# Scatters without the small fill ahead of them, and a new order at the start of the second expert

## The chip, the cores and the metric

The kernel runs on one core of a Trainium2 chip. The metric is the device time of one execution in microseconds (us); a change is read against the median of three runs.

## The reference, cut to what matters

```
# attention: a linear recurrence with decay w, per batch and head (B=4, H=8, S=768, D=48)
for t in range(S):
    y[t]  = r[t] @ (state + (u*k[t]) outer v[t])
    state = w[t][:, None] * state + k[t] outer v[t]
# its output is x: 3072 tokens of 384 values; a router sends each token to one of 8 experts
logits = x @ w_gate;  e = argmax(logits);  g = softmax(logits)[e]
out[token] = g * (relu(x[token] @ w1[e]) @ w2[e])        # w1: 384x1024, w2: 1024x384
```

## The kernel before

**Attention.** 32 iterations (`for i in range(2, NI)`, after a hand-written start), each half a sequence of one pair of heads. The order of each engine's instructions is written by hand; the engines run their own streams in order and meet at semaphores. One iteration on GpSimd (POOL) is `rk` (L444), `diag` (L519, makes SC), `k_mul` (L497, makes Kd), one or two one-element fills that hold back a load (`pace`), in some iterations a scatter, and last `f_out` (L488), which copies 12 columns of the decay product F into `flags`, read much later to tell whether the chunked form was numerically sound. In every second iteration a one-element copy `hint` (L885) follows the scan `states` (L567, makes TT) of VectorE. VectorE runs `decay_l` (L474), `decay_f` (L482), `r_mul` (L500), `sc_out` (L532, which waits for `diag`) and `states`. `decay_l` overwrites a buffer that `k_mul` read, so it waits for GpSimd too.

**Routing.** While batch b+1 is in attention, batch b is routed: its rows are scattered by expert into the DRAM tensor `xs`, 128 rows at a time, by `route_s`: a one-element fill of `spacer` (L277), and an indirect DMA issued by GpSimd (L278). `SCAT` puts 13 of these scatters at the ends of iterations 15 to 20, 23 to 27 and 31 (two of them around the start of iteration 27), 5 behind the last iteration and 6 in the tail, when the last batch is routed. The rows are then read back for the first expert.

**Experts.** Expert 0 has two parts: its first rows are worked off in the attention's tail, the rest (256 rows) afterwards. Experts 1 to 7 (in order of their size) have 464 rows and fewer. The products are made of high and low halves (`H`, `L`) of weights and activations, three matmuls for each. `mm1(e, f)`, f = 0 to 7, makes the hidden block f in one of four PSUM banks (nine matmuls); ScalarE evicts its high half (hH, L1282), VectorE its low half (hL, L1283), and the bank is free when both are done. Then `mm2` (three blocks d, eight f each), whose f-th three matmuls need hH and hL of that f.

For the next expert, in the same time, `xload_` loads its rows (4 DMAs on the SP queue, L1230), `tags` the gate weight and row number of each (4 DMAs of 8-byte pieces, L1217), four DMAs load its weights into four staging buffers (L1057). `xturn` transposes the rows on VectorE (L1240) and `xsplit` makes their halves in three steps, one ScalarE and one VectorE instruction each (L1247, L1248). `W[e+1][2](g)` splits a quarter g of the weights in the same way (L1076, L1078). Where in expert e's blocks `xturn` and the three `xsplit` stand is in `XF`; 8 and up are the blocks of `mm2`. Quarters 0 and 1 of the next expert's w1 are split around the start of `mm2`, quarters 2 and 3 (w2) during the second and third block of `mm2`; only for expert 1 do they stand in its own `mm1`, at f = 1 and f = 4 (`late`).

The issue order on SP around the second expert: weights 0 of expert 1, its rows, weights 1, a zero fill of `xs`, weights 2 and 3, the tags of expert 1; then, with expert 1 started, the rows of expert 2, its tags, its four weights. Loads from `xs` wait for the zero fill.

## Time and profile before

| | |
|---|---|
| median of three runs | 405.98 us (405.19 to 406.72) |
| profiled execution | 406.11 us, of which 404.3 us are the span of its instructions |
| TensorE clock granted | 0.996 of full speed in the mean |
| busy: TensorE, VectorE, GpSimd, ScalarE | 380.5, 293.1, 238.5, 213.5 us |
| attention with its tail; experts | to about 188 us; from there to the end |

Busy time of TensorE contains matmuls that only keep it going (`warm`, `spin`, `pulse`), and the ends of its instructions are modelled, so a stall is read better from the starts of instructions. In a timeline the columns are start (us), duration (us), engine, line, operation, output and inputs, count, and in brackets the idle time of the engine before it and what ended that. PEld is the weight load of TensorE.

### The profile page before, as it was taken

What the parts mean: (1) busy time and instruction counts of PE and PEld (TensorE: products, weight loads), DVE (VectorE), ACT (ScalarE), POOL (GpSimd) and SP (SyncE); (2) the same over time, 40 slices, a digit from 0 to 9 for tenths busy, and PEclk for the clock granted to TensorE, in tenths of its full rate; (3) what the DMA queues carried; (4) which work ended last, traced back from release to release, by engine and by line L of the source; (5) the groups of instructions that cost most, each with busy time, mean ns of one, the idle gap of its engine ahead of it and who ended that gap; (6) DMA issues with size and microseconds to landing.
All of it is one profiled execution on the core that took longest, in us unless ns stands there. A gap on an engine that the chain in (4) does not pass through costs nothing.

```text
span 404.3 us, 13751 instructions
## 1 busy us (share of the span) xinstructions
PE 380.5 (94%) x5546; PEld 338.2 (84%) x5547; DVE 293.1 (72%) x498; ACT 213.5 (53%) x439; POOL 238.5 (59%) x469
## 2 busy tenths in 40 slices
PE   8879999999989989999999999999999999999992
PEld 4567777787767768789988799999999999999992
DVE  7688998888888876567776968787596695864510
ACT  6667668656755764454264564465455554471300
POOL 8655777669976994762120008848748488388211
PEclk9999999999999999999999999999999999999998
DMA  9999998668775954236999769757847576521001
GB/s 141 170 166 157 166 188 179 131 126 174 173 150 123 267 157 147 104 111 192 230 237 212 241 124 357 170 167 209 227 152 183 178 244 175 179 98 37 35 19 40
DMA packets 149039, 66.10 MB, mean 163 GB/s; under 512 B 127774, under 2 KB 140283, under 8 KB 148966
## 3 DMA queue, kind: packets, MB, share of 16 engines
q1 hardware_dynamic: 143030, 55.36, 59.5%
q0 software_dynamic: 4336, 9.47, 6.7%
q8 instruction: 45, 0.74, 0.8%
q10 hardware_dynamic: 1600, 0.30, 0.5%
q14 instruction: 28, 0.23, 0.2%
HBM read 49.72 MB, written 15.87 MB: 162 GB/s over the span
## 4 chain that ended last, share of the span: by engine, by line
PE 64%; DVE 10%; SPq 6%; DMA 6%; POOL 5%; issue 4%; ACT 4%; POOLq 0%; DVEq 0%; ACTq 0%
PE ps L1278 5%; PE pt L1278 5%; PE pk L1265 5%; PE pk L1266 5%; PE pw L1278 5%; PE pp L1278 5%; PE pk L1264 5%; SPq L417 4%; PE both L528 3%; DMA xg<-xs 3%; PE py L596 3%; PE py L1266 3%; PE py L1265 3%; PE py L1264 3%; DVE TT L567 2%
## 5 line engine op out<-in xcount | busy, mean ns | idle before, releaser
L1334 POOL DMA_INDIRECT out_dram<-yo,yi x68 | 85.9, 1264 | 69.4 <-DVE yo L1330 54.7
L1078 DVE TENSOR_TENSOR w2L<-wstage,w2H 128x1536 fp32r<-128x1536 f32 x16 | 33.0, 2060 | 9.1 <-ACT w2H L1076 9.1
L519 POOL TENSOR_TENSOR SC<-eye,qT 128x384 f32<-128x384 f32 x32 | 26.5, 828 | 15.9 <-ACT qT L512 15.6
L278 POOL DMA_INDIRECT xs<-xr,slu x24 | 29.0, 1207 | 8.7 <-DVE slu L272 4.3
L444 POOL TENSOR_TENSOR rk<-rT,kT 112x384 f32<-112x384 f32 x32 | 31.9, 996 | 1.9 <-ACT rT L465 1.9
L1078 DVE TENSOR_TENSOR w1L<-wstage,w1H 128x1536 fp32r<-128x1536 f32 x16 | 28.0, 1756 | 6.8 <-ACT w1H L1076 6.5
L474 DVE TENSOR_TENSOR_SCAN L<-pw,stepb 112x390 f32<-112x390 f32 x30 | 28.7, 956 | 4.6 <-PE pw L453 2.1
L1076 ACT ACTIVATE w2H<-wstage 128x1536 fp32r<-128x1536 f32 x16 | 31.5, 1977 | 0.0
L497 POOL TENSOR_TENSOR Kd<-kT,L 112x384 f32<-112x384 f32 x32 | 29.8, 932 | 1.5 <-ACT kT L469 1.5
L482 DVE TENSOR_TENSOR_SCAN F<-pw,bfw 112x390 f32<-112x390 f32 x30 | 29.0, 968 | 0.9
L516 ACT ACTIVATE Kt<-both 128x288 f32<-128x288 f32 x32 | 13.1, 410 | 31.2 <-PE both L528 30.1
L528 PE MATMUL both<-RF,Kd 48*64 48x112 f32 x768 | 27.9, 262 | 1.6 <-issue 1.6
L1265 PE MATMUL pk<-hL,w2H 128*128 128x464 f32 (+4 forms) x80 | 28.6, 357 | 0.6 <-DVE hL L1283 0.6
L1266 PE MATMUL pk<-hH,w2L 128*128 128x464 f32 (+4 forms) x80 | 28.5, 356 | 0.0
L1264 PE MATMUL pk<-hH,w2H 128*128 128x464 f32 (+4 forms) x80 | 28.4, 355 | 0.0
L532 DVE COPY_PREDICATED SC<-mask,both 128x384 f32<-128x384 uint32 x32 | 19.0, 593 | 11.4 <-POOL SC L519 5.4
L1084 POOL DMA_INDIRECT out_dram<-orow,tag x8 | 9.3, 1160 | 26.8 <-DVE orow L1355 26.3
L567 DVE TENSOR_TENSOR_SCAN TT<-PT,AT 112x576 f32<-112x576 f32 x16 | 22.8, 1425 | 1.2 <-ACT PT L562 1.2
L546 PEld LDWEIGHTS py<-V,Kt 64*48 64x48 f32 x704 | 17.1, 121 | 7.6 <-ACT qT L512 4.8
L1076 ACT ACTIVATE w1H<-wstage 128x1536 fp32r<-128x1536 f32 x16 | 23.5, 1478 | 0.0
L528 PEld LDWEIGHTS both<-RF,Kd 48*64 48x64 f32 x768 | 21.4, 134 | 2.0 <-issue 2.0
L546 PE MATMUL py<-V,Kt 64*48 64x48 f32 x704 | 22.2, 212 | 0.7 <-ACT Kt L516 0.4
(307 smaller groups left out, 1180.5 us busy)
## 6 DMA issues: line engine op xcount, KB each, us to landing
wstage<-in_moe_w_dram SPq DMA_DIRECT2D x28, 768.0 KB
xs<-zrow SPq DMA_DIRECT2D x7, 723.8 KB
in_w<-in_w_dram SPq DMA_DIRECT2D x30, 144.0 KB
in_k<-in_k_dram SPq DMA_DIRECT2D x30, 144.0 KB
in_r<-in_r_dram SPq DMA_DIRECT2D x30, 144.0 KB
V<-in_v_dram SPq DMA_DIRECT2D x15, 168.0 KB
V<-in_v_dram SPq DMA_DIRECT2D x16, 144.0 KB
xg<-xs SPq DMA_DIRECT2D x12, 156.0 KB
```

The source lines that it names most:

```text
L444: nc.gpsimd.tensor_tensor(t[:GP], T["rT", i][:GP], T["kT", i][:GP], op=OP.mult)
L497: nc.gpsimd.tensor_tensor(KDM[i % 3][:GP], chunks(T["kT", i][:GP], C), T["L", i][:, :, 1:], op=OP.mult)
L528: nc.tensor.matmul(psS[half(side, c % 2), side, c // 2, :], KDM[i % 3][kr, c, :], RF[i % 6][kr, c, :], start=True, stop=True)
L546: nc.tensor.matmul(p[64 * side:64 * side + D, par, q, :], T["Kt", i][ts, side, q, :], vat(un, side, par, h * NB + q), start=fresh, stop=fresh)
L567: nc.vector.tensor_tensor_scan(t[:GP].rearrange("p e c -> p (e c)"), PT[un % 2][:GP].rearrange("p e c -> p (e c)"), AT[un % 3][:GP].rearra ...
L1076: nc.scalar.activation(hh, sv, AF.Copy)
L1078: nc.vector.tensor_tensor(ll, sv, hh.bitcast(F32), op=OP.subtract)
L1264: nc.tensor.matmul(p, lh, rh, start=first, stop=False)
L1265: nc.tensor.matmul(p, lh, rl, start=False, stop=False)
L1266: nc.tensor.matmul(p, ll, rh, start=False, stop=last)
L1278: nc.tensor.matmul(p, ws["1" + x][:, c, sl], X[y, e][:, c, :n], start=(j == 0), stop=(j == len(terms) - 1))
L1334: d = nc.gpsimd.indirect_dma_start(out=out.rearrange("n (g x) -> (n g) x", g=XP), out_offset=bass.IndirectOffsetOnAxis(ap=X["i", e][:, q:q ...
```

## The change

Four edits. `route_s` loses the fill of `spacer` (24 times). `f_out` is done by ScalarE in place of GpSimd in those iterations in which a scatter stands. At expert 1, the tags are issued behind the rows of expert 2 in place of ahead of them, and `xturn` and `xsplit` for expert 2 stand at f = 5, 6, 7 and 8 in place of 2, 3, 4 and 5. Quarter 0 of the weights of expert 1 is split after f = 6 of expert 0's `mm1` in place of after f = 7, `xturn` and the first `xsplit`.

```
-XF = ((7,7,8,8),(2,3,4,5))
+XF = ((7,7,8,8),(5,6,7,8),(2,3,4,5))
...
     def route_s(st, q, scat):
-        nc.gpsimd.memset(spacer, 0.0)
         d = nc.gpsimd.indirect_dma_start(
...
-            def f_out(i):
+            def f_out(i, scattered=False):
                 af = flags[:GP, i * NCH * NFS:(i + 1) * NCH * NFS].rearrange("p (c x) -> p c x", x=NFS)
-                nc.gpsimd.tensor_copy(af, T["Fx", i][:, :, 0:C + 1:C // (NFS - 1)])
+                src = T["Fx", i][:, :, 0:C + 1:C // (NFS - 1)]
+                if scattered:
+                    nc.scalar.activation(af, src, AF.Copy)
+                else:
+                    nc.gpsimd.tensor_copy(af, src)
...
                 scatter(i, 1)
                 if nx:
-                    f_out(i + 2)
+                    f_out(i + 2, 2 * i in SC or 2 * i + 1 in SC)
...
             def turn(e, t):
-                for j, at in enumerate(XF[e > 0]):
+                for j, at in enumerate(XF[min(e, 2)]):
...
                     if e:
                         xload_(e + 1, X["src", e + 1])
-                        tags(e + 1, X["src", e + 1] * NR)
+                        for k in range(1 if e == 1 else e + 1, e + 2):
+                            tags(k, X["src", k] * NR)
...
                         W[1][1](2)
                         W[1][1](3)
-                        tags(1, X["src", 1] * NR)
...
                     for at, g, which in late.get(e, ()):
                         if at == f:
                             W[e][2](g, which)
+                    if (e, f) == (0, 6):
+                        W[1][2](0)
                     if nx:
                         turn(e, f)
                 if nx:
-                    W[e + 1][2](0)
+                    if e:
+                        W[e + 1][2](0)
```

## Rows read from the trace of the kernel before

**Rows 1.** Busy time of each engine in the two stretches with scatters between iterations.

```profile
87.70:113.30 25.60, 24.25 (x685) 19.38 (x678) 21.46 (x31) 17.78 (x49) 24.79 (x52) 1.00 0.78 172
127.30:150.40 23.10, 20.47 (x575) 16.34 (x568) 18.57 (x31) 15.25 (x41) 22.23 (x52) 1.00 0.76 204
```

**Rows 2.** Waits of VectorE from 87.7 to 114: total us, times, longest.

```profile
DVE SC L532 <- POOL SC L519: 2.0, 6, 0.5
```

**Rows 3.** Timeline of GpSimd around scatters.

```profile
87.59 0.20 POOL L488 COPY flags<-F 112x12 f32<-112x12 f32 x1
87.72 0.18 POOL L885 COPY hint<-TT 1x1 f32<-1x1 f32 x1
...
90.54 0.09 POOL L277 MEMSET spacer<- 1x1 f32 x1
90.79 1.02 POOL L278 DMA_INDIRECT xs<-xr,slu  x1 [0.16 <-issue]
91.82 0.20 POOL L488 COPY flags<-F 112x12 f32<-112x12 f32 x1
91.98 0.99 POOL L444 TENSOR_TENSOR rk<-rT,kT 112x384 f32<-112x384 f32 x1
...
134.77 1.99 POOL L278 DMA_INDIRECT xs<-xr,slu  x1 [0.16 <-issue]
```

**Rows 4.** Waits of TensorE's weight loads from 204 to 240.

```profile
PEld pk L1265 <- DVE hL L1283: 1.4, 2, 0.8
PEld pw L1278 <- DVE hL L1283: 1.1, 1, 1.1
PEld ps L1278 <- DVE w1L L1078: 0.6, 1, 0.6
...
PEld pk L1266 <- DVE w2L L1078: 0.3, 1, 0.3
```

**Rows 5.** Timeline of TensorE: early rows, end of expert 0, expert 1, start of expert 2.

```profile
186.56 0.52 PE L1122 MATMUL pp<-ident,xr 128*128 128x128 f32 x3 [0.32 <-DMA xr<-xs]
...
200.78 0.33 PE L1266 MATMUL pk<-w2H,hL 128*128 128x384 f32 x1
...
205.15 0.37 PE L1278 MATMUL ps<-xH,w1H 128*128 128x464 f32 x1
...
228.30 0.37 PE L1264 MATMUL py<-hH,w2H 128*128 128x464 f32 x1
...
238.37 0.36 PE L1278 MATMUL ps<-xH,w1H 128*128 128x436 f32 x1
```

**Rows 6.** Timeline of VectorE in two scatter iterations.

```profile
90.60 0.97 DVE L474 TENSOR_TENSOR_SCAN L<-pw,stepb 112x390 f32<-112x390 f32 x1 [0.30 <-POOL spacer L277]
...
134.59 1.35 DVE L567 TENSOR_TENSOR_SCAN TT<-PT,AT 112x576 f32<-112x576 f32 x1
```

**Rows 7.** Groups of ScalarE by line: busy us, mean ns, idle before.

```profile
L512 ACT ACTIVATE qT<-both 128x6 f32<-128x6 f32 x32 | 5.5, 172 | 1.1 <-PE both L528 1.1
```

**Rows 8.** Timeline of VectorE and ScalarE, experts 0 and 1.

```profile
196.67 0.42 DVE L1283 SCALAR_TENSOR_TENSOR hL<-pp,hH 128x256 fp32r<-128x256 f32 x1
...
199.79 2.14 DVE L1240 STREAM_TRANSPOSE xT<-xg 128x1440 f32<-128x1440 f32 x1 [1.99 <-DMA xg<-xs]
...
202.47 1.47 ACT L1076 ACTIVATE w1H<-wstage 128x1536 fp32r<-128x1536 f32 x1
...
203.97 1.76 DVE L1078 TENSOR_TENSOR w1L<-wstage,w1H 128x1536 fp32r<-128x1536 f32 x1 [0.72 <-ACT w1H L1076]
...
217.43 1.98 DVE L1240 STREAM_TRANSPOSE xT<-xg 128x1344 f32<-128x1344 f32 x1 [1.98 <-DMA xg<-xs]
219.33 0.60 DVE L1283 SCALAR_TENSOR_TENSOR hL<-pw,hH 128x464 fp32r<-128x464 f32 x1
...
222.66 2.27 DVE L1078 TENSOR_TENSOR w2L<-wstage,w2H 128x1536 fp32r<-128x1536 f32 x1 [1.43 <-ACT w2H L1076]
```

**Rows 9.** Timeline of the SP queue as expert 1 starts.

```profile
205.60 3.35 SPq L1217 DMA_DIRECT2D tag<-xs  x4
```

## The prediction

> **What bounds the kernel now.** I read the page's busy shares, then the chain that ended last, then each stretch that the diff touches. TensorE has by far the largest share of the chain, so most of the kernel is matmuls that no edit here shortens; what can be won are the places where TensorE stands still or where the attention loop is paced by another engine. There are two such places.

> The first is the loop while scatters run in it. The busy table of the two scatter stretches [rows 1] shows GpSimd filled: 24.79 of 25.60 us and 22.23 of 23.10, and what is missing are the short gaps ahead of each scatter. VectorE has 4.1 and 4.5 us left. TensorE looks as full as GpSimd, but part of its work there is pulses that only keep it going. Who waits decides: VectorE waits for GpSimd's SC in all six iterations of the first stretch, 2.0 us together [rows 2], and before `decay_l` 0.30 us for the buffer that `k_mul` reads [rows 6] (the fill is named there because it ended next; the reader of that buffer is Kd). So an instruction taken from GpSimd in these iterations brings SC and Kd forward, and VectorE with them, up to that wait.

> The second is expert 1. Its first matmul starts at 205.15 and that of expert 2 at 238.37 [rows 5]: 33.2 us for 144 matmuls (72 of `mm1`, 72 of `mm2`). The last 48 of them run from 228.30 to 238.37, 0.21 us each; at that pace 144 take 30.2. So 3.0 us are stalls, and the weight loads' waits name them [rows 4]: the low weights of quarter 0 and low halves hL, all VectorE's work. Why VectorE is late stands in its timeline [rows 8]: `xturn` of expert 2 stands in its stream at f = 2 and waits 1.98 us for rows that aren't there before 217.4, then takes 1.98 us, with hL of f = 3 behind it until 219.33; the four PSUM banks then hold up f = 7. And at the start, quarter 0 of w1 is split behind `xturn` of expert 1, which waited 1.99 us for its rows, so w1L comes at 203.97 + 1.76 = 205.7, later than TensorE's 205.15.

> **The change part by part.** *Flags on ScalarE.* Eleven copies leave GpSimd (iterations 15 to 20 and 23 to 27; in iteration 31 there is none to copy). What one is worth is the distance from its start to the next start: 91.98 - 91.82 = 0.16 where `rk` follows, 87.72 - 87.59 = 0.13 where `hint` follows [rows 3]. Five of the first kind and six of the second: 0.80 + 0.78 = 1.6 us. On ScalarE each costs about 0.17 us, as the copy of 6 columns does [rows 7]; 11 times 0.17 = 1.9 us. They stand at the end of an iteration, and F was made half an iteration before, so they wait for nothing; behind them are the eviction of the next transposes and then the wait for the next `sc`. ScalarE has 25.60 - 17.78 = 7.8 us free in the first stretch, so I take nothing; if that cover is gone the 1.9 us come back.

> *The fill.* It lasts 0.09 us, but instructions of GpSimd overlap at their ends. Bounds: nothing (the gap ahead of the scatter just grows) and 0.09. Of the 13 in the loop the six scatters that meet VectorE's scan of the states gain nothing: at 134.77 a scatter took 1.99 us in place of 1.02 [rows 3], and it was the scan from 134.59, 1.35 long [rows 6], that held it: 135.94 plus some 0.8 is its end. Starting earlier there only waits longer. Six others (the 13th, in iteration 31, stands where GpSimd idles) at 0.05, between the ends: 0.3. With the flags 1.9; the waits of VectorE to be won are a third of a us in an iteration [rows 2, 6] and GpSimd gives back 0.13 to 0.25, so nearly all of it can pass, but not all of it must: I take 1.7, bounds 0 and 2.2 (1.6 + 6 x 0.09).

> [...]

> *The tail.* The six last scatters run one behind another and the rows of the first expert are read back after them; TensorE then waits 0.32 us for these rows [rows 5]. Six fills are 0 to 0.5 us; I take 0.2 of the 0.32. The other five stand ahead of a pause of GpSimd: nothing.

> *Quarter 0 of expert 1 sooner.* The split of 1.47 us on ScalarE and 1.76 on VectorE [rows 8] now stands ahead of the evictions of f = 7 of expert 0. When VectorE takes f = 6's low half at 196.67 its high half is done; so w1H ends by 198.1, w1L by 199.9, hL of f = 7 by 200.3 (0.42). The matmul that needs it starts at 200.78 [rows 5], so it is 0.4 us in time or more. `xturn` of expert 1 starts at 200.3 at the latest in place of 199.79 and ends at 202.5; three steps of about 0.6 each and one eviction of `mm2` follow, to 205.0. The low halves of the rows are used last in f = 0, six matmuls after 205.15, at 206.4. So w1L no longer stalls and xL neither. The cover is that first `mm2` of 8 us; without it the split would cost its 1.76.

> *`xturn` and `xsplit` of expert 2 later.* Without stalls f = 4 ends at 205.15 + 45 x 0.21 = 214.6 and `mm2` starts at 220.3; its last low half is needed 22 matmuls on, at 224.9. ScalarE evicts f = 4 (0.6) and splits quarter 3, as long as VectorE's half, 2.27 [rows 8]: 217.5. VectorE: w2L to 219.8, hL of f = 5 (0.6), `xturn` (1.98) to 222.4, hL of f = 6 to 223.0, xL to 223.6, hL of f = 7 to 224.2. ScalarE's xH and hH of f = 7 lie beside that. That is 0.7 us in time. What is late next is the expert after: its first product now is at some 235, its third xsplit done by some 227.

> *The tags.* Four DMAs, 3.35 us of SP's time [rows 9], move behind the four of expert 2's rows, which so start some 3.4 us sooner than behind them; these were waited for until 217.4, and now nobody asks before 220. Behind the tags are expert 2's tags and its four weights: the same DMAs are ahead of those as before, so they move by nothing, and the last weight's buffer, freed by the split of quarter 3, comes free 5 us sooner (219.8 against 222.66 + 2.27). Expert 1's tags are first used after the first block of `mm2`, about 225, and are issued by about 213.

> For the two edits at expert 1 the stalls of 3.0 us are the upper bound; I take 2.8, as a few evictions may still be met. The lower bound is 1.5, if the start is won only half and one low half is late by its 0.6.

> **Sum.** 406.1 (the profiled execution's own time, 0.1 above the median) - 1.7 - 0.2 - 2.8 = 401.4 us. After expert 1 TensorE runs without a wait into the last expert, so what is won there stays.

> **Rivals.** *A: as summed*, 400.4 to 402.5.

> *B: the loop gives nothing back.* VectorE or TensorE takes over as soon as GpSimd is 0.1 us quicker. For it: TensorE is busy 24.25 of 25.60 [rows 1]. Against: VectorE waits for GpSimd in each iteration [rows 2]. Only tail and experts: 406.1 - 3.0 = 403.1.

> *C: the stall at expert 1 moves.* `xturn` still stands ahead of hL of two blocks, and ScalarE's xH, which waits for it, ahead of hH of f = 7. The margins are 0.7 and 0.4 us, made of durations that overlap. If both are missed by 1 us, and the loop pays: 406.1 - 1.9 - 1.0 = 403.2; if nothing is won at the experts, 404.2.

> *D: slower, by order.* [...] Ahead of the scan, a scatter would hold VectorE, the engine that paces those iterations, for its 1.02 us. The narrowest lead is 134.77 - 134.59 = 0.18 us [rows 3, 6], and the fill is half of that. If all six turned round, the loop would lose 6.1 and win nothing: 406.1 + 6.1 - 3.0 = 409.2; from three of six on it is slower than before. Against it: the scan follows SC by one VectorE instruction, the scatter by Kd as well, and both shift together. [...]

> *E: nothing moves by more than 2 us*, since B and C come together: 405.

> **Chances.** A 0.56, B 0.16, C 0.14, D 0.06, E 0.08. Half a per cent, about what a measurement of this kernel can tell from no change, is 2 us: 404.0 and 408.0. A, B and a part of C lie below 404.0, which with some doubt about the whole gives 0.75; the rest of C, E and a mild D lie between, 0.20; slower 0.05. Range 400.4 to 404.3: the upper end takes in B and most of C, the lower one the upper bounds of every term, 406.1 - 2.2 - 0.3 - 3.0 = 400.6, and a little.

> **What would show it.** In the new profile: no copy of flags on GpSimd between 87 and 113 and the two stretches shorter by some 0.9 and 0.8 us; expert 1's 144 matmuls in 30.2 to 30.5 us, without a wait for hL; VectorE's `xturn` of expert 2 without a wait for rows; rows and tags of SP exchanged. The prediction is wrong if scatters grow longer than 1.02 and 1.99 without the fill, if a scan of the states of over 2 us stands behind a scatter, or if hL of f = 7 is waited for in `mm2` of either expert.

## The result, and the profile after

| | before | after |
|---|---|---|
| median, measured side by side (6 runs each) | 405.59 us (404.10 to 406.72) | 400.55 us (400.05 to 403.04) |
| profiled execution; its span | 406.11; 404.3 us | 400.35; 398.6 us |
| busy: TensorE, VectorE, GpSimd, ScalarE | 380.5, 293.1, 238.5, 213.5 us | 379.3, 292.3, 235.9, 215.0 us |

The ratio is 0.9893, with a 95% interval from 0.9871 to 0.9915: 5.0 us less, where 4.7 were forecast. The median of 400.55 lies in the range of the prediction, 0.15 us above its lower end; not all the terms under it came out.

The table of busy time, laid over the same work as the stretches of [rows 1] (start, end and length, then each engine's busy time):

```profile
87.84:112.90 25.06, 24.35 (x694) 19.40 (x685) 21.50 (x32) 18.19 (x53) 23.98 (x42) 1.00 0.80 177
125.27:147.76 22.49, 20.80 (x591) 16.59 (x583) 18.67 (x31) 15.66 (x45) 21.50 (x42) 1.00 0.80 210
```

GpSimd still fills them, though less tightly: what it lacks is 1.1 and 1.0 us, and was 0.8 and 0.9. Its timeline, which answers to [rows 3]:

```profile
90.66 0.09 POOL L827 MEMSET in_k<- 1x1 f32 x1
90.91 1.02 POOL L277 DMA_INDIRECT xs<-xr,slu  x1 [0.16 <-issue]
91.96 1.01 POOL L443 TENSOR_TENSOR rk<-rT,kT 112x384 f32<-112x384 f32 x1
...
132.53 2.01 POOL L277 DMA_INDIRECT xs<-xr,slu  x1 [0.16 <-issue]
```

No copy of flags stands between scatter and `rk`: 1.05 us from start to start, 1.19 before. The fill is gone too, but little of its 0.09 us is won: from the fill of `pace`, which stands in both kernels, to the scatter it is 0.25 us, and before, with the fill of `spacer` between them, it was 0.27 (to 90.79 in [rows 3]):

```profile
90.52 0.09 POOL L824 MEMSET in_k<- 1x1 f32 x1
```

The scatters are as long as they were.

The scan `decay_l` runs once in each iteration on VectorE, so its starts are a clock of the loop. Before, and then after, at the start of the first stretch, around the space between the stretches, and behind the second:

```profile
86.49 0.94 DVE L474 TENSOR_TENSOR_SCAN L<-pw,stepb 112x390 f32<-112x390 f32 x1
...
108.96 0.97 DVE L474 TENSOR_TENSOR_SCAN L<-pw,stepb 112x390 f32<-112x390 f32 x1 [0.31 <-POOL Kd L497]
114.67 0.95 DVE L474 TENSOR_TENSOR_SCAN L<-pw,stepb 112x390 f32<-112x390 f32 x1
118.78 0.97 DVE L474 TENSOR_TENSOR_SCAN L<-pw,stepb 112x390 f32<-112x390 f32 x1
126.40 0.94 DVE L474 TENSOR_TENSOR_SCAN L<-pw,stepb 112x390 f32<-112x390 f32 x1
...
150.22 0.97 DVE L474 TENSOR_TENSOR_SCAN L<-pw,stepb 112x390 f32<-112x390 f32 x1 [0.30 <-POOL Kd L497]
```

```profile
86.77 0.94 DVE L473 TENSOR_TENSOR_SCAN L<-pw,stepb 112x390 f32<-112x390 f32 x1
...
108.48 0.97 DVE L473 TENSOR_TENSOR_SCAN L<-pw,stepb 112x390 f32<-112x390 f32 x1 [0.30 <-POOL Kd L500]
114.29 0.96 DVE L473 TENSOR_TENSOR_SCAN L<-pw,stepb 112x390 f32<-112x390 f32 x1
118.50 0.95 DVE L473 TENSOR_TENSOR_SCAN L<-pw,stepb 112x390 f32<-112x390 f32 x1
124.49 0.94 DVE L473 TENSOR_TENSOR_SCAN L<-pw,stepb 112x390 f32<-112x390 f32 x1
...
147.58 0.97 DVE L473 TENSOR_TENSOR_SCAN L<-pw,stepb 112x390 f32<-112x390 f32 x1 [0.29 <-POOL Kd L500]
```

Read as after minus before, the clock stands at +0.28 us at the start of the first stretch (86.77 against 86.49), -0.48 behind it (108.48), -0.28 two iterations on (118.50), then at once -1.91 (124.49), and -2.64 behind the second stretch (147.58 against 150.22). So the stretches give 0.76 and 0.73, and 1.63 come in an iteration in which there is no scatter. In that iteration and the one ahead of it TensorE stopped in the kernel before, inside the 24 matmuls of `sc`:

```profile
114.56 0.69 PE L528 MATMUL both<-RF,Kd 48*64 48x112 f32 x17
115.95 0.42 PE L528 MATMUL both<-RF,Kd 48*64 48x112 f32 x7 [0.70 <-issue]
...
119.96 0.41 PE L528 MATMUL both<-RF,Kd 48*64 48x112 f32 x5
121.24 0.79 PE L528 MATMUL both<-RF,Kd 48*64 48x112 f32 x18 [0.88 <-issue]
```

After, the same matmuls (L531 there) run through. At the experts, TensorE, in answer to [rows 5]:

```profile
183.95 0.52 PE L1125 MATMUL pp<-ident,xr 128*128 128x128 f32 x3 [0.26 <-DMA xr<-xs]
...
202.52 0.38 PE L1281 MATMUL ps<-xH,w1H 128*128 128x464 f32 x1
...
217.60 0.37 PE L1267 MATMUL pk<-hH,w2H 128*128 128x464 f32 x1
...
232.73 0.36 PE L1281 MATMUL ps<-xH,w1H 128*128 128x436 f32 x1
```

Expert 1 takes 30.21 us in place of 33.22, and the view of waits shows none of TensorE's weight loads from 196 to 240, where the kernel before had five kinds of wait, four of them in [rows 4]. VectorE, in answer to [rows 8]:

```profile
195.09 1.76 DVE L1081 TENSOR_TENSOR w1L<-wstage,w1H 128x1536 fp32r<-128x1536 f32 x1 [0.65 <-ACT w1H L1079]
196.77 0.42 DVE L1286 SCALAR_TENSOR_TENSOR hL<-pw,hH 128x256 fp32r<-128x256 f32 x1
198.14 2.14 DVE L1243 STREAM_TRANSPOSE xT<-xg 128x1440 f32<-128x1440 f32 x1 [0.95 <-DMA xg<-xs]
...
217.68 1.99 DVE L1243 STREAM_TRANSPOSE xT<-xg 128x1344 f32<-128x1344 f32 x1
...
220.85 0.63 DVE L1286 SCALAR_TENSOR_TENSOR hL<-pw,hH 128x464 fp32r<-128x464 f32 x1
```

`xturn` of expert 2 (217.68) waits for no rows, and hL of f = 7 is done at 221.48; the matmul that reads it starts 22 matmuls after 217.60, at 222.23. On SP, rows and tags have changed places, as against [rows 9]:

```profile
203.93 3.09 SPq L1233 DMA_DIRECT2D xg<-xs  x4
207.22 5.27 SPq L1220 DMA_DIRECT2D tag<-xs  x4
```

### The profile page after: what moved, and what is told of

It reads as the page before. It is cut to its first block, busy times and chain, and to the rows that moved or that the text cites. A ratio compares the mean times of both kernels' runs of the same rounds, so it can differ in the third digit from the quotient of the medians.

```text
span 398.6 us, 13733 instructions
## 1 busy us (share of the span) xinstructions
PE 379.3 (95%) x5546; PEld 339.0 (85%) x5547; DVE 292.3 (73%) x498; ACT 215.0 (54%) x450; POOL 235.9 (59%) x434
## 4 chain that ended last, share of the span: by engine, by line
PE 75%; DVE 7%; POOL 5%; SPq 5%; issue 3%; DMA 3%; ACT 2%; ACTq 0%; POOLq 0%; DVEq 0%
PE ps L1281 7%; PE pp L1281 6%; PE pw L1281 6%; PE pt L1281 6%; PE pk L1267 6%; PE pk L1268 6%; PE pk L1269 6%; SPq L416 3%; PE py L1268 3%; PE py L1267 3%; PE py L1269 3%; PE both L531 3%; PE py L599 3%; DMA in_r<-in_r_dram 2%; DVE TT L570 2%
## 5 line engine op out<-in xcount | busy, mean ns | idle before, releaser
L531 PE MATMUL both<-RF,Kd 48*64 48x112 f32 x768 | 27.2, 261 | 0.0
L599 PE MATMUL py<-TT,RF 48*64 48x48 f32 x656 | 21.8, 265 | 0.7 <-ACT xr L629 0.6
```

The costliest lines, as they stand in the source:

```text
L531: nc.tensor.matmul(psS[half(side, c % 2), side, c // 2, :], KDM[i % 3][kr, c, :], RF[i % 6][kr, c, :], start=True, stop=True)
L599: nc.tensor.matmul(p[side][64 * par:64 * par + 64, q, :], RF[i % 6][kr, c, :C], T["TT", un][kr, :, h * NCH + c], start=(side, par) not in ...
```

## The experiments

Five chips ran them. On four (all but that of e5) TensorE was held back: the kernel before took 437 to 446 us there by the median, at a granted clock of TensorE of 0.950 to 0.977 in the mean of an execution (0.994 to 0.996 on e5's chip). In the profiles of e7 and e10 it was 0.80 in the mean from 160 to 186 us, where the profile before shows 1.00. In this stretch of e7 TensorE stands still for 4.9 us. Three rows: the stretch in the table of busy time, before and in e7 (the clock is the third number from the end), and e7's longest wait of TensorE in it:

```profile
160.00:186.00 26.00, 24.59 (x381) 21.09 (x377) 16.35 (x61) 11.74 (x28) 14.01 (x30) 1.00 0.31 109
```

```profile
160.00:186.00 26.00, 18.93 (x369) 14.85 (x369) 10.96 (x46) 6.80 (x21) 8.71 (x18) 0.80 0.18 63
```

```profile
PE px L603 <- ACT seen L605: 4.9, 1, 4.9
```

Whole times don't resolve the change there: flags alone came out at 1.0041 (0.9956 to 1.0126), 1.0114 (1.0021 to 1.0206) and 0.9887 (0.9797 to 0.9977) of before, and a fourth time without an interval. The changed kernel itself (e9) took 442.88 and 451.71 us there, beside 436.98 to 453.13 of the kernel before. So stages are compared, each as a distance of starts inside one trace. Odd and even: from one `decay_l` to the next, in the first stretch (before: 86.49, 90.60, 95.83, 99.76, 105.00, 108.96); expert 1: from its first matmul to the first of expert 2.

| kernel | odd iterations | even | expert 1 |
|---|---|---|---|
| before | 4.11, 3.93, 3.96 | 5.23, 5.24 | 33.22 |
| after | 3.98, 3.79, 3.80 | 5.07, 5.07 | 30.21 |
| e1, flags alone | 4.00, 3.86, 3.80 | 5.52, 5.77 | 33.72 |
| e6, flags alone | 4.00, 3.87, 3.81 | 5.53, 5.78 | 33.22 |
| e10, flags alone | 4.00, 3.85, 3.81 | 5.52, 5.82 | 31.29 |
| e11, flags alone | 3.99, 3.85, 3.81 | 5.55, 5.82 | 32.21 |
| e2, fill alone | 4.11, 3.94, 3.95 | 5.27, 5.69 | 33.83 |
| e8, fill alone | 4.12, 3.95, 3.95 | 5.32, 5.72 | 32.15 |
| e3, experts alone | 4.12, 3.93, 3.96 | 5.30, 5.73 | 30.21 |
| e7, experts alone | 4.12, 3.93, 3.96 | 5.33, 5.73 | 30.21 |
| e4, without quarter 0 | 4.12, 3.94, 3.96 | 5.28, 5.73 | 30.84 |
| e5, stream moved | 4.13, 3.93, 3.95 | 5.23, 5.24 | 32.78 |
| e9, the changed kernel | 4.00, 3.86, 3.80 | 5.52, 5.78 | 30.39 |
| e12, scan later | 3.60, 3.24, 3.24 | 5.83, 6.17 | 30.38 |

Expert 1 without its edits took 31.29 to 33.83 us, with all of them 30.21 to 30.39. So the 3.0 us are what they win in the profile before; in another execution it can be less, 31.29 (e10) being the least that was met.

**Flags alone (e1, e6, e10, e11).** Fill, quarter 0, `xturn` and tags as before.

```
-                    f_out(i + 2)
+                    f_out(i + 2, 2 * i in SC or 2 * i + 1 in SC)
```

> Only the flags' copies move to ScalarE; fill, quarter 0, xturn and tags as before. Theory 1 (GpSimd paces these iterations, a copy is worth the distance to the next start): the two scatter stretches together are 1.4 to 1.6 us shorter, so 404.0 to 404.2 against 405.6. Theory 2 (the two stops of TensorE inside the sc matmuls near 116 and 121 us, 0.9 and 1.1 us, which the changed kernel doesn't show, go away because these iterations come earlier): another 1.6 us, 402.5 to 402.6, with no stop of over 0.5 us in sc. Rival (the shorter loop is only this second effect): the stretches as long as before, 404.0 with the stops gone or 405.6 with them there. Expert 1 takes 33.2 us as before.

> Only the flags' copies move to ScalarE, on a chip where the kernel before shows its usual clock. Theory 1 (each of the 11 copies gives GpSimd back 0.12 to 0.16 us and VectorE follows): 1.3 to 1.6 us less from the two scatter stretches. Theory 2 (TensorE's two stops at instructions 5824 and 6080 come and go with the place of the work between two fetches): this edit adds no instruction to TensorE, so the stops stay at a remainder of 192, but they are short or absent since the iterations around them come 0.7 us earlier: 1.6 us more, 402.4 to 402.7 against 405.6. If the stops stay as long as before: 404.0 to 404.3. Rival (GpSimd was not what paced the stretches): 405.6, or 404.0 by the stops alone.

> Only the flags' copies move to ScalarE, once more, since on two chips TensorE was held back in these stretches (even iterations of 5.7 us in place of 5.2) and the loop won nothing in its even iterations. Theory 1 (where TensorE runs as in the profile before, GpSimd paces the stretches): 0.6 to 0.8 us less in each stretch, as in the changed kernel. Theory 2: the stops at TensorE's instructions 5824 and 6080 are gone or under 0.3 us, another 1.3 to 1.6 us. Both: 402.4 to 402.9 against 405.6; theory 1 alone 404.0 to 404.4; neither (rival B of the prediction, TensorE takes over): 405.6. Expert 1 stays at 32.5 to 33.2 us in each case.

> Only the flags' copies move to ScalarE. What is open is whether GpSimd paces the two scatter stretches where TensorE is at the clock of the profile before. Theory 1 (it does): the odd iterations are 0.1 us shorter as on the two other chips and the even ones too, 0.6 to 0.8 us in each stretch, 404.0 to 404.4 against 405.6. Theory 2 on top of it (the stops at instructions 5824 and 6080 are gone in this execution): 402.4 to 402.9. Rival B of the prediction (TensorE takes over in the even iterations, as on the two chips where they were 5.5 to 5.8 us long): under 0.5 us, 405.2 or more.

In all four the odd iterations are shorter by 0.07 to 0.16 us. The even ones are longer than without the edit on the same chips (5.52 to 5.55 against 5.27 to 5.33): TensorE pauses in them, as e7 shows in the second one of the stretch, though no wait stands there, and GpSimd, which waits for nothing but the issue of its scatters in these iterations of the profile before, waits 0.4 us for `qT`, made from TensorE's `both`:

```profile
100.61 0.56 PE L507 MATMUL both<-ucol,rk 48*64 48x1 f32 x20
101.33 0.19 PE L507 MATMUL both<-ucol,rk 48*64 48x1 f32 x1 [0.17 <-issue]
```

From the first to the sixth `decay_l` that makes 22.95 to 23.02 us, against 23.03 to 23.07 in e3, e4 and e7: some 0.1 us at most. On those chips the first stretch does as rival B said. In the second one the same edit is worth 0.2 us or a little more: from the `decay_l` that answers to 126.40 to that of 139.79, 13.39 to 13.43 us in place of 13.62 to 13.69. Where TensorE isn't held back, before and after differ by 0.16 and 0.17 in the even iterations too, 21.71 against 22.47. No run had the flags' edit alone on such a chip. That the 0.76 and 0.73 are theirs for the most part rests on GpSimd's own spacing, 0.14 us less behind the scatter and 0.02 less ahead of it, and on the next experiment.

**Fill alone (e2, e8).**

```
     def route_s(st, q, scat):
-        nc.gpsimd.memset(spacer, 0.0)
```

> Only the fill ahead of each scatter is taken out. The prediction's term: 6 x 0.05 in the loop and 0.2 at the tail, 0.5 us together, so 405.1 against 405.6. Theory from the changed kernel's trace (the gap ahead of a scatter grows to take the fill's place): 0.0 to 0.1 us, 405.5 to 405.6; spacing of the last scatters 1.27 to 1.28 us. If the two stops of TensorE inside sc (0.9 and 1.1 us) hang on where the loop stands, they stay, since the loop moves by under 0.1 us.

> Only the fill ahead of each scatter is taken out. The prediction's term: 0.3 us in the loop and 0.2 at the tail. Theory from the changed kernel's trace (the gap ahead of a scatter takes the fill's place): the six last scatters 1.27 to 1.28 us apart as before, the loop's decay_l within 0.1 us of before at 114.7, apart from what TensorE's stops do; 405.5 against 405.6.

Odd and even iterations are those of e3, e4 and e7 to within 0.04 us, and the six last scatters are 1.27 to 1.30 us apart, in e3 1.27 to 1.29. And e9, which has the flags' edit and no fill, is within 0.01 us of e6, flags alone on the same chip. So no worth of the fill shows, in the loop or in the tail. The whole times, 0.9929 (0.9871 to 0.9988) and 1.0135 (0.9982 to 1.0288), point both ways and settle nothing.

**The experts' edits alone (e3, e7)**: XF, tags and quarter 0 as in the change, the rest as before.

> The three edits at the experts alone (quarter 0 sooner, xturn of expert 2 later, tags behind the rows); the loop as before. Theory: expert 1's 144 matmuls in 30.2 us in place of 33.2 and the time 3.0 us less, 402.6 against 405.6, with no wait of the weight loads between 196 and 240. Rival (part of what is won at the experts needs the earlier rows of the shorter loop): 31 us or more and 403.4 or later. The two stops of TensorE inside sc should be those of the kernel before, since nothing ahead of them changes; if they are missing here, they are a matter of the single execution.

> The three edits at the experts alone. Theory: the loop is as before, expert 1's 144 matmuls take 30.2 us in place of 33.2, no weight load waits between 196 and 240 us: 402.6 against 405.6. Rival (part of the gain needs the earlier rows of the shorter loop): 31 us or more and 403.4 or later. TensorE's stops at 5824 and 6080 stay, 0.7 and 0.9 us, as nothing ahead of them changes.

The first theory, to the hundredth: 30.21 us in both, and no wait of a weight load in the stretch. Nothing of the gain needs the shorter loop. Whole time: 0.9893 (0.9830 to 0.9956) and 0.9965 (0.9875 to 1.0055).

**Without quarter 0 (e4).** XF and tags as in the change; this part undone:

```
-                    if (e, f) == (0, 6):
-                        W[1][2](0)
```

> xturn of expert 2 at f = 5 to 8 and the tags behind the rows, but quarter 0 of w1 split where it was before. Theory by the prediction's two causes: the start of expert 1 still waits for w1L and the low half of the rows (0.5 to 0.8 us), the wait in its f = 3 to 7 is gone (2.2 to 2.5 us): 30.7 to 31.0 us for its 144 matmuls, 403.1 to 403.4 against 405.6. Rival (the late start passes on: VectorE begins expert 1 late and one hL of its last products is late by 0.6 us or more): 31.3 us or more, 403.7 or later.

30.84 us: the earlier split is worth 0.63, the later `xturn` and tags the other 2.4 of the 33.22 in the profile before. The whole time is 0.9940 (0.9892 to 0.9988). The waits of the weight loads name what is left at the start, and nothing later:

```profile
PEld ps L1278 <- DVE w1L L1078: 0.5, 1, 0.5
PEld ps L1278 <- DVE xL L1248: 0.3, 1, 0.3
```

**TensorE's stream moved (e5).** On the kernel before:

```
             warm(WARM[0])
+            for _ in range(64):
+                nc.tensor.matmul(pyt[:1, :1], ones[:, :1], ones[:, :1], start=True, stop=True)
```

> The kernel before with 64 matmuls of one column, a weight load each, put ahead of TensorE's first work: 128 instructions more on TensorE and nothing else changed. In the trace of the kernel before TensorE stops in the sc matmuls at 115.95 + 0.42 and 121.24 us, and the record that follows each stop is instruction 5824 and 6080 of TensorE's stream: both leave 192 when divided by 256, and the instruction queue moves 16 KB at a time, 256 instructions of 64 bytes. Theory (TensorE has run out of instructions and waits for the next 16 KB): no stop is left inside sc after 7 and 18 of 24 matmuls; the stops that remain come 64 matmuls earlier in the work, again at a remainder of 192 in the longer stream, and the loop from decay_l near 114.7 to the one near 126.4 takes 10.0 to 11.7 us. Rival (something else stops TensorE there, such as the loads that fill the DMA engines): the stops stay where they are in the work, inside sc, at a remainder of 64 now, and the stretch takes 11.7 us.

The starts of TensorE's instructions were numbered in the order of time, loads and matmuls together, and every weight load listed that waits for no semaphore and starts more than 0.1 us after the end of what was ahead:

```
kernel   start us   stopped us   number   remainder by 256
before     40.34      0.12        1472       192
before     78.72      0.27        3776       192
before    115.95      0.70        5824       192
before    121.24      0.88        6080       192
after      36.08      0.18        1216       192
after      40.63      0.28        1472       192
after      79.09      0.44        3776       192
after     142.95      0.31        7360       192
e5         44.29      0.50        1729       193
e5        138.90      0.13        7105       193
```

(e5's records hold one more at the head, so 193 there is 192.) All ten stops stand at a step of 256 instructions, and the trace has one transfer of the queue `q8 instruction`, 16,384 bytes, for each such step: in the profiles before and after, 24 of them land between instructions 1216 and 7360, one in each of the 24 steps (the 64 bytes of the expectation are 16,384 / 256, an estimate from this), and the whole profile before lists 45, 0.74 MB, for TensorE's 11,180 instructions. Their times go with the stops: each of the ten ends 1.2 to 1.6 us after one has landed, those at 115.95 and 121.24 after landings at 114.53 and 119.74. On the four held-back chips the same list has 4 to 11 stops for each profile, and 1 to 3 of them stand at a step; the others are the pauses told of above.

In e5 the steps lie at other places of the work, and its two stops are at steps by the new count, not where the kernel before had any: they follow the count. `sc` runs through:

```profile
117.62 0.79 PE L528 MATMUL both<-RF,Kd 48*64 48x112 f32 x24
...
122.72 0.79 PE L528 MATMUL both<-RF,Kd 48*64 48x112 f32 x22
```

and from the `decay_l` that answers to 114.67 to that of 126.40 it is 10.19 us in place of 11.73:

```profile
117.72 0.95 DVE L474 TENSOR_TENSOR_SCAN L<-pw,stepb 112x390 f32<-112x390 f32 x1
121.92 0.96 DVE L474 TENSOR_TENSOR_SCAN L<-pw,stepb 112x390 f32<-112x390 f32 x1
127.91 0.94 DVE L474 TENSOR_TENSOR_SCAN L<-pw,stepb 112x390 f32<-112x390 f32 x1
```

So some 1.5 us of the profile before were these two stops, in `sc` of two iterations; that TensorE waited there for its next instructions is inferred from their places in the stream and from the landings 1.42 and 1.50 us ahead of their ends. It doesn't take a moved stream to be without them: e2, e3, e4, e7 and e8 have the stream and the loop of the kernel before, or that loop without the fill, and none has a stop at 5824 or 6080, which was expected of e3 and e7. All five ran on held-back chips. So did e1, e6, e10 and e11, which therefore can't show whether the flags' edit takes the stops away. The kernel of e5 as a whole is slower, 1.0073 (1.0031 to 1.0116), as the 64 matmuls push the loop back by 3.0 us.

**The scan behind the scatter (e9, e12).** On the changed kernel, meant for the six places where a scatter and the scan of the states meet:

```
                 if even and i > 2:
+                    if 2 * i - 1 in SC:
+                        for _ in range(7):
+                            nc.vector.memset(held, 0.0)
                     states(un - 1)
```

> The changed kernel with seven small VectorE fills (59 ns each) ahead of the scan of the states in the six iterations where a scatter meets it. In the changed kernel the scan starts 0.16 to 0.66 us ahead of the scatter, takes 1.35 to 1.59 us, and the scatter is stretched to 1.75 to 2.01. Rival D of the prediction (whoever starts first holds the other): where the fills are longer than that lead the scatter is 1.02 long, the scan is stretched by 0.5 to 1.0 us and VectorE's next scan is as late, 1 us per turned iteration on top of the fills' 0.4. Its rival (VectorE is never held by a scatter, only the scatter by VectorE): the scan stays at 1.35 to 1.6 us, the iterations lose 0.4 us each at most and the kernel is at 400.5 to 403.0.

> The changed kernel with seven VectorE fills (59 ns each, some 0.4 us) ahead of the scan of the states in the six iterations where a scatter meets it; the run before this one had them under a condition that never came true. In the changed kernel the scan starts 0.39, 0.56, 0.65, 0.36, 0.16 and 0.66 us ahead of its scatter, lasts 1.35 to 1.59, and the scatter 1.75 to 2.01. Rival D of the prediction (whoever starts first holds the other for its length): where the order turns, at 0.39, 0.36 and 0.16 at the least, the scatter lasts 1.02 and the scan 1.9 to 2.4 us; three turned iterations cost 3 us, or less what GpSimd wins by the shorter scatters. Its rival (a scatter never holds VectorE): the scan stays at 1.35 to 1.6 us whichever starts first, and the six iterations lose 0.4 us each at most, 2.4 us together. TensorE's stream is the changed kernel's: stops, if any, at a remainder of 192.

In e9 the condition was `2 * i in SC`, which names the other half of the iteration and never came true: e9 is the changed kernel itself, and its odd iterations and expert 1 confirm it. In e12 the order turned in all six places. VectorE, then GpSimd, at the narrowest place of [rows 3, 6]:

```profile
137.15 0.68 DVE L890 MEMSET held<- 128x1 f32 x6
137.88 1.35 DVE L571 TENSOR_TENSOR_SCAN TT<-PT,AT 112x576 f32<-112x576 f32 x1
```

```profile
137.25 1.01 POOL L278 DMA_INDIRECT xs<-xr,slu  x1 [0.16 <-issue]
```

The scatter starts 0.63 us ahead, in the others 0.13 to 0.41; each scan lasts 1.35 us, each scatter 1.01 to 1.20 in place of 1.75 to 2.01. Of these two the first to start did not hold the other both ways: a scan that was ahead held the scatter, a scatter that was 0.13 to 0.63 us ahead didn't hold the scan. The profile of the kernel before already had this order once, in iteration 31 (GpSimd, then VectorE):

```profile
163.75 1.04 POOL L278 DMA_INDIRECT xs<-xr,slu  x1 [0.27 <-DVE slu L272]
```

```profile
163.96 1.34 DVE L567 TENSOR_TENSOR_SCAN TT<-PT,AT 112x576 f32<-112x576 f32 x1
```

The loop as a whole wins nothing by it. The first five distances of the table add to 22.08 us, 0.9 less than in e9, but they leave out the cost of the fills in the iteration just ahead, where the first place lies: with that iteration it is 28.86 us against 28.94, and over the four distances that answer to those from 118.78 to 139.79 in the profile before, with two such places, 19.83 against 19.39. The fills take 0.7 us at each place, so the order gives back most of what they cost, and not more. Against before the whole is 0.9987 (0.9924 to 1.0049).

## Why the prediction was right, step by step

- **Flags, 1.6 us of the term: right.** The stretches are 0.76 and 0.73 shorter, 1.49 (some 0.9 and 0.8 were forecast for flags and fill together), and fill alone gave none of that where it was run. GpSimd did pace them, and VectorE followed nearly 1 to 1. In the two iterations behind the first stretch 0.2 were given back.
- **The fill, 0.3 in the loop and 0.2 at the tail: wrong, 0.** The lower bound was the value: the gap ahead of a scatter takes the fill's place. The step that failed is the 0.05 us taken between the bounds: by the prediction's own measure, from start to next start, the fill of `pace` (90.52) and that of `spacer` (90.54) lie 0.02 apart, and with one of them gone the other is followed by the same gap of 0.25. TensorE's wait for the early rows went from 0.32 [rows 5] to 0.26 us, and the shift of the loop is the same before and after the tail (-2.64 and -2.61).
- **Quarter 0 sooner: right.** The quarter's high half started as soon as hH of f = 6 was out (193.58), and hL of f = 7 was done at 197.19, 0.9 us ahead of the matmul that reads it (198.15); forecast 0.4 or more. Worth 0.63 (e4).
- **`xturn`, `xsplit` and tags: right, size too.** 2.4 us; the margin of hL of f = 7 in expert 1 was some 0.7 us, as forecast. The experts gave 3.0, the upper bound, where 2.8 was taken: no eviction was met.
- **What the sum lacked:** TensorE's stops at the steps of 256 instructions. [Rows 2] were read to find who waits for GpSimd, and two rows of TensorE without a releaser, 0.70 and 0.88 us, were not asked about. The page has them as `1.6 <-issue 1.6` behind the 768 matmuls of `sc`; on the page after, 0.0 stands there. They lay outside the places that the diff touches, and the loop lost 1.6 us by them. By the terms alone the profile would have been at 406.11 - 1.49 + 0.2 - 3.0 = 401.8. It was 400.35: 1.63 by stops that are gone, less 0.28 lost ahead of the stretches, where the changed kernel has three stops of 0.90 us together and the kernel before two of 0.39; 0.1 is left over. So the mechanisms of the sum came to 4.3 us where 4.7 were added up, and that the median moved by 5.0 and still lies in the range is luck: more than 1 us of the profile's gain was in no term.
- **Rival B** did not happen in the profiles before and after, and did in the first stretch on the held-back chips, where TensorE's pauses (0.17 us in the rows of e7) are the difference that the rows show. **Rival C** did not: its margins held. **Rival D** could not have happened at these leads: e12 turned the order in six places, and no scan became longer. That a scatter ahead of the scan would hold VectorE was a supposition: no run shows it, nor the 6.1 us that the loop was to lose by it. The rows picked out have the scan ahead, but the trace of the kernel before has the other order once: the scan at 163.96 stands behind the scatter at 163.75 and takes 1.34 us, which could have settled this rival beforehand. The runs show one direction only: with the scan ahead the scatter takes 1.72 to 2.04 us, with the scatter 0.13 to 0.63 us ahead the scan takes 1.35. Where a scan of the profile before is longer, another instruction of GpSimd is under way: three of the six in the profile before take 1.58 to 1.60 us, and there `k_mul` had begun 0.55 to 0.58 us ahead.

Open: why the transfers for instructions 5824 and 6080 came late in the profile before and in time after. They were no slower than others (1.09 and 1.15 us, where all take 0.9 to 1.6 between 30 and 150 us), but began 2.46 and 2.64 us after TensorE had passed the step before; of the 80 steps in that stretch of the profiles before, after and e5, five have over 2.1 us there, and all five are stops. What holds these transfers back isn't shown: the edits shift the work against the transfers of the other queues (on the page of the profile before `q1` has 59.5% of the 16 DMA engines' time, `q8 instruction` 0.8%), but no run varied these alone. Nor is it shown that the change takes these stops away; they are missing in other profiles of the loop before. Open too is whether a scan that starts just behind the scatter, at less than the 0.7 us of e12's fills, makes the changed kernel faster; no run on a chip without TensorE's pauses had it.

## What to carry to other kernels

Cost an instruction of a filled engine by the distance to the next start, and count it only where the other engines of that iteration wait for it: the flags paid 0.07 to 0.17 us each, the fill nothing. A stop of TensorE that no semaphore explains is worth numbering by its place in the stream: here ten lay whole multiples of 256 instructions apart and came and went from one profile to the next, and two of them, 0.70 and 0.88 us, are in the profile before and not in that after. A distance from start to start that gets shorter can be paid for just outside its ends, as in e12. Where one engine's instruction holds another's, one order may be free: here VectorE's scan, 0.13 to 0.63 us behind the scatter, took 1.35 us and the scatter 1.01 to 1.20, where with the scan ahead the scatter took 1.75 to 2.01.
